# Running sums of eight groups from two float32r parts: GatedLoop attention with a SoLU feed-forward, one Trainium2 core

## The chip, the cores and the metric

The kernel runs on one core of one Trainium2 chip. The metric is the device time of a whole execution in microseconds (us). The time before is the median of three executions.

## The reference

For 4 batches, 8 heads, 768 steps and head dimension 48, a complex gate `a` is cut to a modulus of at most 0.999 and drives a linear recurrence; the real part of the state is read with `q`. The result (3072 tokens of 384) goes through a feed-forward block with a softmax-gated activation and a layer norm.

```python
scale = np.minimum(mag, 0.999) / (mag + 1e-06)
a_re_n, a_im_n = a_re * scale, a_im * scale
for t in range(S):
    new_re = ar * S_re - ai * S_im          # ar, ai: a_re_n, a_im_n at step t
    new_im = ar * S_im + ai * S_re
    S_re, S_im = new_re + k[t] (x) v[t], new_im
    y[t] = q[t] . S_re
h = x @ w_in                                # x: y, heads side by side; 3072x384 @ 384x1024
solu = h * softmax(h)
ln = (solu - mean) / sqrt(var + 1e-06) * g_ln
out = ln @ w_out                            # 1024x384
```

## The kernel before

The sequence is cut into 6 blocks of 128 steps. A block of one batch is a chunk; there are 24 chunks, numbered c, and two chunks of neighbouring batches are a group g, of which there are 12 (g counts from 0, so "group 5" of the title is g = 4). Within a block the recurrence is unrolled: the logarithm of the gate's modulus and its angle are summed along the 128 steps, which turns the recurrence into a masked product of scaled and rotated q and k.

The work is made of small named steps, and each is a closure that issues one or a few instructions:

- Preparation of a group, on tiles of 128 partitions by 768 (`prep_steps`): `inverse`, `ratio`, `sure`, `tangent`, `square`, `secant`, `fourth`, `size`, `eps` and `lnm` compute the tangent of the angle in tile `x0` and the logarithm in tile `lr`. They alternate between ScalarE (ACT) and VectorE (DVE). `total` then sums `lr` along the 128 steps by a matrix product with a triangle of ones (`tri`); `grow` and `decay` (ACT) take the exponential of the sum with both signs. After a load of the trigonometric table (`trig`), `angle` takes the arctangent, `on` (DVE) adds the phase carried over from the block before, and `phase` sums `x0` by a product with the triangle scaled by -0.5/pi (`turns`). `nearest`, `part`, `sin` and `cos` follow, and `exp` loads the exponential table again. `total` and `phase` are done for each chunk of the group (index 0 and 1). `ks` and `qs` scale k and q (DVE).
- Rotation of a chunk (`turn_steps`): `q2` and `k2` (DVE), a blockwise transpose `kqb` (DVE) and four DMAs `kqt0` that complete it.
- Attention of a chunk (`chunk_steps`): `score0/1` on TensorE (PE), `mask0` (DVE), `values` (PE), and `carry` (PE) with `add` (DVE) for the state.
- Feed-forward of a chunk (`ffn_steps`): `turned_x` (ACT copy), `up0/1` (PE), `exp0` (ACT), `solu0` (DVE), `blocks` (DVE transpose) and `away` (DMAs), `centred` (POOL, that is GpSimd), `spread` (ACT), `norm` (POOL), `down0/1` (PE), `scale` (ACT), `store` (DMA). Chunks 0, 1, 2 and 23 transpose with PE instead (`zt`, `zT`).
- Weights: `fetch`, `raised`, `convert` turn the 64-bit weights into float32; `again` fetches each of the seven pieces a second time and `inspect` (DVE) looks for values that are too small.

Nothing is scheduled at run time. A text, `ORDER`, lists all steps in one sequence, and each engine and the DMA queue on SyncE (SP) executes its own instructions in that order; semaphores bind the engines to each other. Tiles come from pools: the scratch tiles `lr`, `x0` and `u` have one buffer each, so the preparation of group g+1 can't overwrite them before group g has read them; the pool `raw`, which holds fetched weights, has three buffers; PSUM for `total`, `phase` and the transposes has two banks, and the accumulators f_y, f_h and f_o have one buffer each.

Every product has float32 operands. Most are cut into four instructions of 32 stationary columns that write 32 output partitions each, and the four run in the array side by side. The trace has two records of each float32 product. The running sums are issued so (line 846):

Of the kernel before, what the change touches and what calls it, by code (L numbers as in the profile page):

```python
# [11 lines left out]
FP = mybir.dt.float32  # L12
I32 = mybir.dt.int32
# [502 lines left out]
load_ara:0 inversea:0 load_aia:0 ratioa:0 surea:0 load_arb:0 tangenta:0 inverseb:0 squarea:0 load_aib:0 secanta:0  # L516
fourtha:0 ratiob:0 sureb:0 sizea:0 fetch:5 epsa:0 tangentb:0 squareb:0 secantb:0 lnma:0 fetch:1 raised:5 load_k:0
sizeb:0 fetch:0 epsb:0 total0:0 convert:5 load_q:0 fourthb:0 raised:1 grow0:0 decay0:0 lnmb:0 total1:0 grow1:0 fetch:2
decay1:0 convert:1 trig:0 anglea:0 angleb:0 ks1:0 phase0:0 phase1:0 load_vr:0 raised:0 convert:0 nearest0:0 nearest1:0
load_ar:1 part0:0 cosa:0 sina:0 qs0:0 qs1:0 load_ai:1 part1:0 ks0:0 sinb:0 fetch:6 cosb:0 q2:0 last:0 exp:0 qt0:0  # L520
qT0:0 raised:2 k2:0 qt1:0 qT1:0 kt0:0 kt1:0 load_v:0 q2:1 convert:2 kT0:0 inverse:1 fetch:3 fetch:4 gain:0 kT1:0 qt1:1
raised:6 k2:1 score0:0 onward:0 kt0:1 qT1:1 score1:0 turn_ends:0 ratio:1 kT0:1 load_k:1 sure:1 mask0:0 tot:0 tangent:1
values:0 convert:6 square:1 turned_x:0 secant:1 fourth:1 qt0:1 raised:3 size:1 convert:3 eps:1 qT0:1 load_q:1 lnm:1
up1:0 up0:0 raised:4 exp0:0 convert:4 total1:1 total0:1 grow1:1 ks1:1 decay0:1 grow0:1 decay1:1 trig:1 kt1:1 load_ar:2
angle:1 carry:1 kT1:1 phase0:1 ks0:1 load_ai:2 qs0:1 last:1 nearest0:1 solu0:0 phase1:1 nearest1:1 part0:1 score1:1
part1:1 score0:1 sin:1 mask0:1 zt1:0 qs1:1 cos:1 add:1 mean:0 load_q:2 mean:1 exp:1 mean:3 zT1:0 q2:2 values:1 k2:2
mean:7 inverse:2 load_v:1 mean:5 mean:4 mean:2 turned_x:1 mean:6 turn_ends:1 kqb:2 ratio:2 meansum:0 carry:0 up0:1
kqt0:2 centre:6 zt0:0 tot:1 sure:2 centred:0 centre:5 tangent:2 centre:7 square:2 up1:1 score0:2 score1:2 secant:2
spread:0 centre:4 centre:1 centre:0 size:2 zT0:0 k2:3 eps:2 centre:2 centre:3 down0:0 load_vr:1 fourth:2 q2:3 lnm:2
total1:2 exp0:1 total0:2 kqb:3 decay0:2 grow1:2 load_k:3 grow0:2 mask0:2 add:0 decay1:2 trig:2 down1:0 load_k:2  # L530
solu0:1 angle:2 on:2 values:2 kqt0:3 onward:1 zt0:1 centred:1 qs0:2 turned_x:2 zT0:1 carry:2 phase1:2 phase0:2 last:2
load_ar:3 nearest0:2 norm:0 score0:3 score1:3 ks1:2 nearest1:2 part0:2 scale:0 part1:2 sin:2 add:2 up1:2 cos:2
load_ai:3 up0:2 mask0:3 ks0:2 exp:2 q2:4 k2:4 inverse:3 values:3 exp0:2 load_v:2 turn_ends:2 load_q:3 zt1:1 kqb:4
ratio:3 zT1:1 solu0:2 turned_x:3 sure:3 down0:1 centred:2 tangent:3 kqt0:4 down1:1 tot:2 spread:1 square:3 zt1:2
secant:3 zt0:2 qs1:2 size:3 up1:3 carry:3 zT0:2 q2:5 k2:5 load_vr:2 fourth:3 eps:3 up0:3 store:0 norm:1 scale:1
score1:4 lnm:3 zT1:2 kqb:5 total1:3 add:3 total0:3 onward:2 exp0:3 load_ar:4 score0:4 down0:2 decay0:3 decay1:3
grow1:3 mask0:4 grow0:3 load_k:4 solu0:3 kqt0:5 qs0:3 centred:3 down1:2 blocks:3 spread:2 trig:3 angle:3 values:4 on:3
turned_x:4 phase1:3 phase0:3 last:3 norm:2 ks0:3 nearest0:3 carry:4 nearest1:3 part0:3 load_v:3 score1:5 ks1:3 away:3
part1:3 score0:5 add:4 up1:4 sin:3 cos:3 scale:2 qs1:3 exp:3 store:1 load_ai:4 spread:3 load_q:4 up0:4 mask0:5
turn_ends:3 inverse:4 q2:6 values:5 k2:6 kqb:6 exp0:4 ratio:4 turned_x:5 solu0:4 sure:4 tangent:4 down0:3 norm:3  # L540
kqt0:6 down1:3 centred:4 square:4 blocks:4 carry:5 secant:4 size:4 up1:5 tot:3 store:2 k2:7 eps:4 q2:7 scale:3 up0:5
score1:6 lnm:4 score0:6 onward:3 kqb:7 exp0:5 away:4 total1:4 load_vr:3 fourth:4 load_ar:5 total0:4 down0:4 decay0:4
solu0:5 grow1:4 grow0:4 mask0:6 decay1:4 trig:4 kqt0:7 centred:5 qs0:4 angle:4 down1:4 blocks:5 add:5 spread:4 on:4
store:3 values:6 away:5 phase0:4 last:4 turned_x:6 phase1:4 norm:4 ks0:4 nearest0:4 carry:6 nearest1:4 part0:4 part1:4
add:6 score0:7 sin:4 score1:7 ks1:4 up1:6 scale:4 up0:6 mask0:7 qs1:4 load_ai:5 turn_ends:4 spread:5 load_q:5 down0:5
cos:4 q2:8 values:7 exp:4 k2:8 inverse:5 kqb:8 exp0:6 ratio:5 load_k:5 down1:5 turned_x:7 solu0:6 sure:5 tangent:5
kqt0:8 carry:7 square:5 blocks:6 secant:5 norm:5 away:6 load_vr:4 fourth:5 up0:7 size:5 up1:7 k2:9 eps:5 q2:9
centred:6 score0:8 tot:4 score1:8 lnm:5 total0:5 kqb:9 scale:5 total1:5 load_v:4 exp0:7 decay0:5 down0:6 grow1:5
grow0:5 mask0:8 decay1:5 solu0:7 kqt0:9 qs0:5 down1:6 add:7 centred:7 spread:6 values:8 blocks:7 trig:5 angle:5
onward:4 on:5 last:5 phase0:5 turned_x:8 norm:6 phase1:5 away:7 ks0:5 nearest0:5 carry:8 nearest1:5 up1:8 part1:5  # L550
part0:5 store:5 scale:6 add:8 score0:9 sin:5 cos:5 score1:9 ks1:5 qs1:5 load_ar:6 load_ai:6 spread:7 load_q:6 up0:8
mask0:9 q2:10 values:9 exp:5 k2:10 kqb:10 down0:7 exp0:8 inverse:6 ratio:6 down1:7 turned_x:9 solu0:8 sure:6
turn_ends:5 kqt0:10 norm:7 tangent:6 square:6 blocks:8 store:4 carry:9 secant:6 size:6 up1:9 load_vr:5 fourth:6 up0:9
k2:11 tot:5 eps:6 q2:11 score0:10 centred:8 away:8 score1:10 lnm:6 exp0:9 total0:6 kqb:11 scale:7 total1:6 load_k:6
load_v:5 add:9 spread:8 decay0:6 down0:8 grow0:6 mask0:10 decay1:6 solu0:9 grow1:6 trig:6 kqt0:11 ks1:6 qs0:6 down1:8
centred:9 onward:5 values:10 blocks:9 away:9 angle:6 on:6 turned_x:10 norm:8 phase1:6 last:6 phase0:6 nearest0:6 ks0:6
part0:6 carry:10 nearest1:6 part1:6 up1:10 store:7 add:10 score0:11 sin:6 cos:6 score1:11 up0:10 mask0:11 scale:8
k2:12 q2:12 kqb:12 exp:6 load_ar:7 down0:9 load_ai:7 spread:9 load_q:7 exp0:10 inverse:7 ratio:7 values:11 down1:9
turned_x:11 sure:7 solu0:10 turn_ends:6 tangent:7 square:7 norm:9 blocks:10 qs1:6 kqt0:12 carry:11 secant:7 store:6
add:11 size:7 up1:11 load_vr:6 fourth:7 eps:7 up0:11 away:10 k2:13 q2:13 centred:10 score0:12 load_v:6 exp0:11 tot:6  # L560
score1:12 lnm:7 total0:7 kqb:13 scale:9 total1:7 grow1:7 decay0:7 down0:10 grow0:7 mask0:12 decay1:7 solu0:11 load_k:7
trig:7 angle:7 store:8 spread:10 qs0:7 centred:11 down1:10 kqt0:13 blocks:11 values:12 on:7 last:7 phase0:7
turned_x:12 norm:10 phase1:7 onward:6 scale:10 up1:12 carry:12 nearest1:7 nearest0:7 ks0:7 part1:7 away:11 part0:7
add:12 score0:13 sin:7 cos:7 score1:13 ks1:7 up0:12 mask0:13 exp:7 k2:14 q2:14 load_ar:8 load_ai:8 spread:11 kqb:14
load_q:8 exp0:12 inverse:8 ratio:8 down0:11 values:13 sure:8 down1:11 turned_x:13 solu0:12 kqt0:14 turn_ends:7
tangent:8 square:8 blocks:12 qs1:7 onward:7 secant:8 carry:13 norm:11 store:10 away:12 size:8 up1:13 load_vr:7
fourth:8 k2:15 q2:15 eps:8 up0:13 score0:14 centred:12 tot:7 scale:11 exp0:13 score1:14 lnm:8 total1:8 total0:8 kqb:15
grow1:8 decay0:8 down0:12 load_v:7 grow0:8 mask0:14 decay1:8 solu0:13 load_k:8 load_ar:9 kqt0:15 centred:13 qs0:8
spread:12 down1:12 add:13 trig:8 values:14 store:11 angle:8 turned_x:14 blocks:13 norm:12 on:8 away:13 store:9 last:8
phase0:8 phase1:8 ks0:8 nearest0:8 load_ai:9 spread:13 carry:14 nearest1:8 part0:8 up1:14 load_q:9 part1:8 score1:15  # L570
ks1:8 add:14 score0:15 sin:8 cos:8 norm:13 exp:8 up0:14 mask0:15 k2:16 scale:12 q2:16 down0:13 kqb:16 exp0:14
inverse:9 ratio:9 values:15 down1:13 turned_x:15 solu0:14 sure:9 turn_ends:8 kqt0:16 tangent:9 square:9 blocks:14
qs1:8 secant:9 carry:15 scale:13 up1:15 size:9 load_vr:8 fourth:9 eps:9 up0:15 q2:17 k2:17 centred:14 score0:16 tot:8
# [37 lines left out]
def whole(ctx, tc, flag, q, k, v, a_re, a_im, moe_w_in, moe_w_out, moe_g_ln, out):  # L611
# [179 lines left out]


    def prep_steps(g):
        ti, b0 = g * GB // B, g * GB % B

        class Tiles(dict):
            def __missing__(self, nm):
# [138 lines left out]
        if ti > 0:  # L936
            own["on"] = on
        if ti < NC - 1:
            own.update(turn_ends=turn_ends, tot=tot, onward=onward)
# [379 lines left out]
```

## Time and profile before

| | |
|---|---|
| Time, median of 3 | 422.66 us (422.07 to 425.59) |
| Profiled execution, its own time | 421.44 us |
| Its span | 419.1 us |
| PE busy | 381.9 us (91%) |
| DVE busy | 331.8 us (79%) |
| ACT busy | 287.5 us (69%) |
| POOL busy | 57.0 us (14%) |
| Running sums on PE (line 848), busy | 38.4 us |

The profile is of one execution. A busy time is the union of an engine's instructions; "PEld" is the load of the stationary operand, which runs beside the products. Instruction groups are named by source line, engine, operation and tile (output<-inputs). `f_L` is the output of `total`, `f_phase` that of `phase`, `f_h` of `up`, `f_o` of `down`, `f_y` of `values`, `f_d` of `carry`, `f_zt` of the transposes on PE. The shape "128*32" of a product means 128 rows by 32 columns of the stationary operand.

### The profile page before, as it was taken

Reading aid. Unit: us, or ns where it says so; the run is one execution under the profiler, and the core shown is the slowest. Engines: PE = TensorE matmul, PEld = TensorE weight load, DVE = VectorE, ACT = ScalarE, POOL = GpSimd, SP = SyncE. Lnnn points to the kernel's source line nnn. Section 1 sums busy time; section 2 is a strip of 40 time slices with the busy share of each in tenths; the row PEclk is TensorE's granted clock in tenths of the full one; section 3 lists DMA queues with packets and bytes.
Section 4 is the critical chain, followed back from the end, with each engine's and each line's share of the span. In section 5 each row is a group of like instructions: output and inputs, shape, how many; then the busy total and the mean of one; then the engine's idle time right before and its main releaser. Section 6 shows DMA issues by size and latency. Waiting matters only on the chain.

```text
span 419.1 us, 15795 instructions
## 1 busy us (share of the span) xinstructions
PE 381.9 (91%) x6928; PEld 200.4 (48%) x6928; DVE 331.8 (79%) x429; ACT 287.5 (69%) x468; POOL 57.0 (14%) x139
## 2 busy tenths in 40 slices
PE   0258779999999999999999999999999999999993
PEld 0025344555554554554555555555455544545441
DVE  4899899788799689699699599689798798774550
ACT  5898978888577768677667767866866885621440
POOL 3000000321210201021211211102111111010210
PEclk9988999999999999999999999999999999999998
DMA  8999436875858738769589857788868869478970
GB/s 235 311 262 215 86 83 127 180 159 113 194 137 173 176 93 179 151 149 206 122 191 201 176 125 157 189 180 192 167 141 196 167 156 204 94 170 256 328 260 28
DMA packets 167261, 72.58 MB, mean 173 GB/s; under 512 B 142480, under 2 KB 155792, under 8 KB 166416
## 3 DMA queue, kind: packets, MB, share of 16 engines
q1 hardware_dynamic: 167040, 71.17, 72.3%
q8 instruction: 56, 0.92, 0.9%
q10 hardware_dynamic: 144, 0.33, 0.3%
q14 instruction: 21, 0.17, 0.1%
HBM read 38.87 MB, written 4.72 MB: 104 GB/s over the span
## 4 chain that ended last, share of the span: by engine, by line
PE 79%; ACT 9%; DMA 4%; DVE 3%; issue 2%; SPq 0%; POOL 0%; DVEq 0%; ACTq 0%; POOLq 0%
PE f_o L1162 28%; PE f_h L1085 26%; PE f_y L1044 9%; PE f_score L1011 5%; PE f_phase L848 4%; PE f_L L848 4%; PE f_d L1052 3%; DMA f_ar<-in_a_re_dram 2%; DMA f_raw<-in_moe_w_out_dram 1%; DMA f_kqT<-f_kb 1%; PE f_zt L1112 1%; ACT f_cs L912 1%; ACT L946 1%; DVE f_kb L966 1%; ACT f_cs L907 1%
## 5 line engine op out<-in xcount | busy, mean ns | idle before, releaser
L1085 PE MATMUL f_h<-f_w_in,f_xT 128*32 128x512 f32 x1152 | 130.7, 593 | 0.4 <-ACT f_xT L1078 0.4
L1162 PE MATMUL f_o<-f_w_out,f_zT 128*32 128x384 f32 (+1 forms) x1344 | 130.1, 486 | 0.3 <-ACT f_zT L1117 0.2
L1162 PEld LDWEIGHTS f_o<-f_w_out,f_zT 128*32 128x32 f32 (+1 forms) x1344 | 55.0, 114 | 64.9 <-issue 55.0
L1085 PEld LDWEIGHTS f_h<-f_w_in,f_xT 128*32 128x32 f32 x1152 | 39.7, 110 | 64.8 <-issue 64.0
L966 DVE STREAM_TRANSPOSE f_kb<-f_kq 128x1536 f32<-128x1536 f32 x22 | 56.0, 2544 | 2.6 <-DMA f_kqT<-f_kb 2.2
L1095 ACT ACTIVATE f_z<-f_h 128x1024 f32<-128x1024 f32 x24 | 28.6, 1193 | 15.5 <-PE f_h L1085 15.5
L1078 ACT COPY f_xT<-f_y 128x384 f32<-128x384 f32 x24 | 11.4, 474 | 39.8 <-PE f_y L1044 39.8
L1011 PEld LDWEIGHTS f_score<-f_kqT 96*32 96x32 f32 x1536 | 32.7, 111 | 10.4 <-issue 9.8
L1044 PE MATMUL f_y<-f_att,f_v 128*32 128x128 f32 (+1 forms) x384 | 36.1, 273 | 1.2 <-DVE f_att L1016 1.2
L1104 DVE SCALAR_TENSOR_TENSOR f_z<-f_h,f_z 128x1024 f32<-128x1024 f32 (+1 forms) x36 | 33.4, 962 | 3.9 <-ACT f_z L1095 3.9
L1044 PE MATMUL f_y<-f_att,f_vr 128*32 128x128 f32 x384 | 36.4, 273 | 0.0
L1140 POOL TENSOR_SCALAR f_less<-f_sum 128x1 f32<-128x1 f32 x24 | 13.1, 546 | 163.4 <-DVE f_z L1104 152.7
L1016 DVE TENSOR_TENSOR f_att<-f_score,f_mats 128x1024 f32<-128x1024 f32 x24 | 29.1, 1213 | 7.2 <-PE f_score L1011 7.2
L903 DVE SCALAR_TENSOR_TENSOR f_f<-f_f,f_phase 128x384 f32<-128x384 f32 x24 | 13.0, 552 | 26.8 <-ACT f_f L899 26.5
L848 PE MATMUL f_L<-f_lr,f_mats 128*32 128x384 f32 x192 | 19.3, 518 | 15.7 <-DVE f_lr L843 15.7
L1011 PE MATMUL f_score<-f_kqT 96*32 96x32 f32 (+3 forms) x1536 | 32.8, 236 | 0.0
L1044 PE MATMUL f_y<-f_kqT,f_state 96*32 96x128 f32 (+1 forms) x640 | 32.7, 272 | 0.0
L1143 ACT ACTIVATE f_z<-f_z,f_less 128x1024 f32<-128x1024 f32 x24 | 27.5, 1147 | 0.0
L1166 ACT ACTIVATE f_ot<-f_o,f_rs 128x384 f32<-128x384 f32 x24 | 13.7, 573 | 16.5 <-POOL f_rs L1151 6.0
L1044 PEld LDWEIGHTS f_y<-f_att,f_v 128*32 128x32 f32 (+1 forms) x384 | 21.8, 103 | 6.2 <-issue 3.8
L1122 DVE STREAM_TRANSPOSE f_zb<-f_z 128x1024 f32<-128x1024 f32 x20 | 24.8, 1238 | 0.1
L957 DVE TENSOR_TENSOR f_kq<-f_cs,f_q 128x768 f32<-128x768 f32 x24 | 22.9, 952 | 2.2 <-ACT f_cs L912 1.1
(101 smaller groups left out, 585.2 us busy)
## 6 DMA issues: line engine op xcount, KB each, us to landing
f_kqT<-f_kb SPq DMA_DIRECT2D x88, 192.0 KB, 3.4
f_zT<-f_zb SPq DMA_DIRECT2D x80, 128.0 KB, 3.2
f_raw<-in_moe_w_out_dram SPq DMA_DIRECT2D x16, 384.0 KB, 5.1
f_raw<-in_moe_w_in_dram SPq DMA_DIRECT2D x6, 1024.0 KB, 7.7
f_k<-in_k_dram SPq DMA_DIRECT2D x12, 384.0 KB, 5.2
f_q<-in_q_dram SPq DMA_DIRECT2D x12, 384.0 KB, 5.4
f_v<-in_v_dram SPq DMA_DIRECT2D x12, 384.0 KB, 5.0
out_dram<-f_ot SPq DMA_DIRECT2D x24, 192.0 KB, 3.7
```

Of the source, the lines that this page charges most:

```text
L848: nc.tensor.matmul(out=ps[r:r + 32], lhsT=weights[:, r:r + 32], rhs=st[nm][:, i * DM:(i + 1) * DM], start=True, stop=True)
L957: nc.vector.tensor_tensor(out=t, in0=T["cs", g][:, i * H:(i + 1) * H], in1=heads(T[nm, g][:, i]).unsqueeze(2).to_broadcast([P, H, 2, D]), ...
L966: nc.vector.transpose(out=t, in_=T["kq", c].rearrange("p n h (f j) -> p j (n h) f", j=3))
L1011: nc.tensor.matmul(out=scores[r0:r0 + 32, x, r:], lhsT=QK[:, r // 32, x], rhs=QK[:, r // 32:, H + x], start=True, stop=True)
L1016: nc.vector.tensor_tensor(out=st["att"].rearrange("p (i u) t -> p i u t", u=2), in0=scores.rearrange("p (i u) t -> p i u t", u=2), in1=mat ...
L1044: nc.tensor.matmul(**product)
L1085: nc.tensor.matmul(out=st["h"][r:r + 32, half * 512:(half + 1) * 512], lhsT=st["xT"][:, c * P + r:c * P + r + 32], rhs=w_in[:, c, half * 5 ...
L1095: nc.scalar.activation(out=z, in_=h, func=AF.Exp, accum_out=sums[:, n:n + 1])
L1104: nc.vector.scalar_tensor_tensor(out=z, in0=h, scalar=1.0, in1=z, op0=OP.mult, op1=OP.mult, accum_out=st["sum"][:, 2 + i:3 + i])
L1122: nc.vector.transpose(out=st["zb"], in_=st["z"].rearrange("p (c s f) -> p s c f", s=4, f=32))
L1143: nc.scalar.activation(out=st["z"], in_=st["z"], func=AF.Square, bias=st["less"], accum_out=st["sum"][:, 1:2])
L1162: nc.tensor.matmul(out=st["o"][rows], lhsT=zT, rhs=w_out[:, c], start=(c == 0), stop=(c == KF - 1))
```

## The change

For the groups g = 4 to 11 the summed tile is split into two parts in the type float32r, and each running sum is one product of the whole 128-column triangle with the first part and a second that accumulates the rest, in place of four products of 32 columns in float32. Both sums use the triangle of ones; the factor -0.5/pi of the phase goes into the split. `lh` and `xh` make the first part on ACT, into the buffer of `u`; `ll` makes the rest of the logarithm on POOL and `xl` that of the phase on DVE, both into buffers of `raw`. Groups 0 to 3 are computed as before. `ORDER` is written anew over its whole length: two of the repeated fetches of weights (`again:5` and `again:0`) stand early, `load_ai` of a group stands ahead of `load_ar`, and most steps keep their neighbours or move by a few places. On PE a group's steps stand in the same sequence as before, except that a `score` comes ahead of `carry` after each `phase`.

```diff
+FR = mybir.dt.float32r
...
+        split = g >= 4
...
+        def high(nm, src, by):
+            t = st[nm] = tmp.tile([P, GW], FR, tag="u", name="f_" + nm)
+            nc.scalar.activation(out=t, in_=st[src], func=AF.Copy, scale=by)
+
+        def low(nm, src, hi, by):
+            t = st[nm] = rawp.tile([P, 1024], FR, tag="raw", name="f_" + nm)
+            if by == 1.0:
+                nc.gpsimd.tensor_tensor(out=t[:, 0:GW], in0=st[src], in1=st[hi].bitcast(FP), op=OP.subtract)
+            else:
+                nc.vector.scalar_tensor_tensor(out=t[:, 0:GW], in0=st[src], scalar=by, in1=st[hi].bitcast(FP), op0=OP.mult,
+                                               op1=OP.subtract)
+
+        def halves(ps, i, *parts):
+            for k, nm in enumerate(parts):
+                nc.tensor.matmul(out=ps, lhsT=tri.bitcast(FR), rhs=st[nm][:, i * DM:(i + 1) * DM], start=(k == 0),
+                                 stop=(k == len(parts) - 1))
...
-            running(ps, i, tri, "lr")
+            if split:
+                halves(ps, i, "lh", "ll")
+            else:
+                running(ps, i, tri, "lr")
...
-            running(ps, i, turns, "x0")
+            if split:
+                halves(ps, i, "xh", "xl")
+            else:
+                running(ps, i, turns, "x0")
...
+        if split:
+            c = -0.5 / math.pi
+            own.update(lh=partial(high, "lh", "lr", 1.0), ll=partial(low, "ll", "lr", "lh", 1.0),
+                       xh=partial(high, "xh", "x0", c), xl=partial(low, "xl", "x0", "xh", c))
```

One period of the order, from one `exp` to the next, as each engine sees it, for g = 9:

```
before
ACT  exp:8 scale:12 exp0:14 inverse:9 turned_x:15 sure:9 square:9 secant:9 scale:13 fourth:9 eps:9 tot:8 exp0:15
     grow0:9 decay0:9 grow1:9 decay1:9 trig:9 angle:9 spread:14 turned_x:16 nearest0:9 nearest1:9 part0:9 scale:14
     part1:9 sin:9 spread:15 cos:9 exp:9
DVE  mask0:15 k2:16 q2:16 kqb:16 ratio:9 solu0:14 tangent:9 blocks:14 qs1:8 size:9 q2:17 k2:17 lnm:9 kqb:17 mask0:16
     solu0:15 qs0:9 add:15 blocks:15 on:9 ks0:9 part0:9 part1:9 add:16 ks1:9 mask0:17 k2:18 q2:18
POOL centred:14 centred:15 norm:14
PE   up0:14 down0:13 values:15 down1:13 turn_ends:8 carry:15 up1:15 up0:15 score0:16 score1:16 total1:9 total0:9
     down0:14 down1:14 values:16 phase0:9 phase1:9 carry:16 up1:16 score0:17 score1:17 up0:16
after
ACT  exp:8 spread:13 inverse:9 exp0:14 sure:9 turned_x:15 square:9 secant:9 fourth:9 eps:9 lh:9 spread:14 scale:13
     tot:8 exp0:15 grow0:9 decay1:9 decay0:9 grow1:9 trig:9 angle:9 xh:9 turned_x:16 nearest0:9 nearest1:9 part0:9
     part1:9 sin:9 cos:9 scale:14 exp:9
DVE  mask0:15 k2:16 q2:16 kqb:16 ratio:9 solu0:14 tangent:9 blocks:14 qs1:8 size:9 k2:17 lnm:9 q2:17 kqb:17 add:15
     mask0:16 solu0:15 on:9 blocks:15 xl:9 qs0:9 ks0:9 ks1:9 part0:9 part1:9
POOL norm:13 centred:14 ll:9 norm:14 centred:15
PE   down0:13 values:15 down1:13 turn_ends:8 carry:15 up1:15 score1:16 up0:15 score0:16 total1:9 total0:9 down0:14
     down1:14 values:16 phase0:9 phase1:9 score0:17 carry:16 score1:17 up0:16
```

## The prediction

> **What bounds the kernel now.** I read the engine totals, then the clock row, then busy time by stretch, then the chain of waits in order of time.
>
> ```profile
> span 419.1 us, 15795 instructions
> PE 381.9 (91%) x6928; PEld 200.4 (48%) x6928; DVE 331.8 (79%) x429; ACT 287.5 (69%) x468; POOL 57.0 (14%) x139
> ...
> PEclk9988999999999999999999999999999999999998
> ```
>
> The stretches, columns PE, PEld, DVE, ACT, POOL:
>
> ```profile
> 100.00:405.00 305.00, 304.81 (x5877) 160.11 (x5866) 243.68 (x293) 201.27 (x327) 43.97 (x104) 1.00 0.75 176
> 405.00:419.00 14.00, 6.82 (x30) 3.90 (x26) 3.97 (x9) 3.30 (x6) 1.80 (x7) 0.91 0.15 51
> ```
>
> From 100 to 405 us PE is idle for 0.2 us, at full clock. Work taken off PE there is time off the end, provided nothing else becomes late. The chain (start, duration) gives the price of a running sum and of a change of tile shape:
>
> ```profile
> 86.24 0.59 PE f_zt L1112 x4
> 86.82 5.16 PE f_o L1162 x16
> 91.99 0.87 PE f_zt L1112 x8
> 92.86 2.71 PE f_h L1085 x24
> ...
> 101.23 5.36 PE f_o L1162 x16
> ...
> 118.81 5.16 PE f_o L1162 x64
> ...
> 130.91 1.29 PE f_L L848 x16
> ```
>
> A pair of sums (both chunks) costs 1.29 us in the steady part, 0.645 us each: 384 columns at four array cycles each, at the 2.4 GHz that the Trainium skill's "TensorE: Matmul & The Clock Gate", Part 1, gives for a busy array. The f_o of 16 records is the 128-column shape, that of 64 the four-tile shape; both take 5.16 us, so a 128-column load hides. The eight transposes of 128 columns take 0.87 us, 0.109 us each, so it hides even there. Entering the wide shape from tiles costs about 0.2 us (5.36 against 5.16; 0.59 against 0.43 for four transposes), leaving it 0.13 us (2.71 against 2.58).
>
> How close the preparation is to being late is read from the timeline at the logarithm's end (L843) and the sum that follows:
>
> ```profile
> 127.55 0.96 DVE L843 SCALAR_TENSOR_TENSOR f_lr<-f_lr,f_u 128x768 f32<-128x768 f32 x1 [0.24 <-ACT f_u L840]
> 130.73 1.47 PE L848 MATMUL f_L<-f_lr,f_mats 128*32 128x384 f32 x16
> ...
> 283.63 0.96 DVE L843 SCALAR_TENSOR_TENSOR f_lr<-f_lr,f_u 128x768 f32<-128x768 f32 x1 [0.39 <-ACT f_u L840]
> 284.64 1.50 PE L848 MATMUL f_L<-f_lr,f_mats 128*32 128x384 f32 x16
> ```
>
> Over the eight groups the slack between the two is 2.2, 1.1, 0.6, 0.05, 0.6, 0.05, 1.0 and 0.5 us, 0.76 in the mean. From the end of `on` (L891) to `phase` it is 0.2 to 1.9 us. PE is the bound, but the preparation is a second chain just under it. DVE (16 of 20 us) and ACT (13 of 20) have room in sum.
>
> **What the Trainium skill says.** "FP8 and Floating Point Precision", TensorE Precision Notes: true float32 takes four passes, while the reduced form reads 4 bytes and truncates to 22 bits. The four cycles a column above agree with the first; no trace here shows the second. I estimate from it one pass, 384 / 2.4 = 0.16 us a product. "TensorEngine Tiling (Array Packing)", Key Properties: a change of tiling mode drains the array; the 0.2 and 0.13 us above agree. "GPSIMD Engine Reference", 3.1: a float32 tensor_tensor of 2048 elements takes 4497 ns; scaled to 768, I estimate 1.69 us for `ll`. "SBUF — State Buffer", "SBUF: two separate sides": GpSimd and a DVE instruction with two SBUF inputs exclude each other. The trace agrees: POOL's L1150 took 1.56 us at 291.66, against 0.22 elsewhere, while DVE ran L891 and L872, both of two inputs, until 293.15.
>
> **The change part by part.**
>
> *Products.* 8 groups x 2 = 16 pairs. Removed: 16 x 1.29 = 20.6 us. Added per pair: four products of 0.16 us = 0.64, plus one entry and exit, 0.33, together 0.97; 16 x 0.97 = 15.5 us. Saved: 5.1 us; I take 4.9, since entering in the middle of a group cost 0.24 once (f_o at 68.12, after scores). Bounds: at half the entry cost, 7.5 us saved; if a float32r column takes two cycles and not one, a pair is 1.29 + 0.33 and 5.3 us are lost.
>
> *`lh`, `ll` ahead of `total`.* `lh` is an ACT pass over 128x768, 0.84 us (row L826); `ll` 1.69 us on POOL, bounded by 0.95 (the same shape on DVE, L836) and 3.0 (1.69 plus the 1.34 that L1150 waited). With 0.1 for semaphores that is 2.6 us in a chain with 0.76 to spare, so it must start earlier. In g = 9 the old table load ends at 269.13, but `inverse` starts at 271.56, behind `scale`, a wait for f_h of 0.82 and `exp0`; `ratio` waits 1.19 for the DMA of f_ai. In the new order only `spread` (1.14) is between, and f_ai is loaded ahead of f_ar: about 2.5 us regained, `lnm` done near 282.1, `lh` 283.0, `ll` 284.7. PE arrives 0.3 us earlier than before, 284.3, and reaches the second part 0.36 us later. It just fits. Behind `ll` on POOL stands `norm`, which `scale` needs only before the next `down` pair, over 5 us later.
>
> *`xh`, `xl` ahead of `phase`.* After `lh` ACT has `spread`, `scale`, `tot` and `exp0` (2.9 us), so `grow` starts near 285.9; four exponentials take 1.64, the table 1.28, `angle` 0.85, `on` 0.9, `xh` 0.84. `blocks` (1.24, on DVE behind `on`) ends after that, then `xl` 0.96: ready near 292.7. PE, after 0.97 + 5.16 + 1.76 and the first part, is there at 292.55. A wait of 0.15 us a group, 1.2 us in all. Behind the waiting product on PE stand `score`, `carry` and `up`, everything. If the cover is gone, each late us is paid in full, because the next preparation starts only after this `phase` has freed `x0` and `u`. Other groups have other neighbours; I bound this wait by 0 and 0.8 us a group.
>
> *DVE and ACT load.* 0.96 and 1.7 us more per group of 30.7 us, on 25 and 22: hidden in sum.
>
> *Raw buffers.* `ll` and `xl` use two of three while `again:5` holds the third until late: the pair is free again after its product, a group earlier than needed. Nothing.
>
> *Head and tail.* Groups 0 to 3 compute the same; the first 60 us (PE idle for half of them, the DMA share 0.95 and 0.99 in the first 40) have a new order with the same transfers. I take 0, within 2 us either way. At the end `judges` (L1208 to L1210, 0.45 us at 402.33) now stands behind `solu0:23` instead of ahead, and two of seven repeated fetches are gone: 0.5 us gained, 0 if `down:22` covers it.
>
> Sum: -4.9 + 1.2 - 0.5 = -4.2; 421.44 - 4.2 = 417.2. The profiled execution is 0.3% under the median of 422.66; the same 4.2 from the median is 418.5, and I put the forecast at 417.3. Under 1%, 4.2 us, a measurement of this kernel can't be told from no change.
>
> **The rivals.**
>
> 1. *The main line*, 415 to 420, chance 0.45. For it: PE idle 0.2 of 305 us. A third of it lies over 418.4, the 1% bound.
> 2. *The new order does better*: shape changes at half price (another 2.6 us) and a shorter head (1 to 2): 413. Chance 0.12. For it: the head has 30 us of PE idling. Against: it is tied to transfers.
> 3. *The preparation becomes the bound*: 0.6 us a group of waiting at `phase` rather than 0.15. -4.9 + 4.8 - 0.5: 420.8. Chance 0.22. For it: the slacks of 0.05 us. Against: idle of ACT at the old `inverse`.
> 4. *The other side: `ll` is slow.* Place: POOL between `lnm` and `total`. If it takes 3.2 us, held out by `k2`/`q2` on DVE, PE waits 1.5 us at each of eight totals, which `phase` passes on: -4.9 + 12 - 0.5 = +6.6: 428. It decides from 2.2 us on, where the wait of 0.5 with that at `phase` eats the saving. Chance 0.13, from 422.5 to 430.
> 5. *float32r isn't a single pass*: +5.3 + 1.2 - 0.5: 427.4. Chance 0.08. The loss would lie in the products themselves, with no waits.
>
> **How the numbers follow.** Faster by over 1%: 0.30 + 0.12 + 0.08 (the part of 3 whose head is short) = 0.50. Within 1%: 0.15 + 0.14 = 0.29. Slower: 0.13 + 0.08 = 0.21. The range 411.5 to 426.5 holds 1 to 3 and the near half of 4. The likeliest case's own range is 415 to 420.
>
> **What would show it.** Right: f_L and f_phase of the split groups as records of 128*128 with starts 0.16 us apart, a pair near 0.97 us in the chain, periods between phases near 30.1 us instead of 30.7. Wrong: PE waits on POOL's `ll` (4), on DVE's `xl` (3), products twice as long (5). A head that ends elsewhere than near 60 us would mean that the order and not the split moved the time.

## The result, and the profile after

The changed kernel takes 421.81 us in the median (420.46 to 424.49), against 423.0 us for the kernel before in the same series (421.04 to 428.58). The ratio is 0.997, 95% interval 0.9948 to 0.9992: a gain of about 0.3%, below the 1% that I asked of a change to be told from none. The profiled execution took 421.55 us, 0.1 more than that of before.

Engine totals and clock row of the changed kernel:

```profile
span 419.7 us, 15441 instructions
...
PE 381.2 (91%) x6736; PEld 207.8 (50%) x6736; DVE 339.8 (81%) x437; ACT 301.0 (72%) x484; POOL 70.7 (17%) x147
...
PEclk9956999999999999999999999999999999999999
```

PE lost 192 records (6928 to 6736) and 0.7 us of busy time, where the sums alone should have given 4 to 5. The clock row has a 5 and a 6 in its first tenth, where before had two 8s: the trace's clock records (when the granted clock changed, and to what share) have it at half for 17.1 us there, and for 6.8 us before. The stretch from 100 to 405 us, columns PE, PEld, DVE, ACT, POOL, then the granted clock:

```profile
100.00:405.00 305.00, 304.77 (x5752) 167.43 (x5748) 255.81 (x298) 218.17 (x350) 58.48 (x111) 1.00 0.76 177
```

PE is idle for only 0.2 us, as before, though DVE has 12 and ACT 17 us more to do there: no wait for `ll` or `xl`. The chain of waits (start, duration) has the new pairs:

```profile
136.37 0.90 PE f_L L863 x4
137.28 5.30 PE f_o L1192 x64
...
144.33 0.90 PE f_phase L863 x4
```

A pair takes 0.90 us instead of 1.29, and the f_o behind it 5.30 instead of 5.16. The two rests that feed it, by form (busy us, mean ns of one, then idle before them):

```profile
L856 POOL TENSOR_TENSOR f_ll<-f_lr,f_lh 128x768 fp32r<-128x768 f32 x8 | 15.5, 1933 | 53.9 <-ACT f_lh L851 53.9
L858 DVE SCALAR_TENSOR_TENSOR f_xl<-f_x,f_xh 128x768 fp32r<-128x768 f32 x8 | 7.2, 903 | 0.0
```

I cut the span at the phase sums of groups 1, 3 and 11 (start of the first record in the timeline). Before: 50.16, 108.30, 353.83, end 419.1. After: 51.78, 113.73, 355.15, end 419.7.

| part of the span, us | before | after | difference |
|---|---|---|---|
| start to phase of g = 1 | 50.16 | 51.78 | +1.62 |
| g = 1 to g = 3 (the middle of the head) | 58.14 | 61.95 | +3.81 |
| g = 3 to g = 11 (all the split sums but the last `phase` pair) | 245.53 | 241.42 | -4.11 |
| g = 11 to the end (the tail) | 65.27 | 64.55 | -0.72 |

So the part that the sums were to shorten is shorter by about the amount forecast, and the head, in which groups 0 to 3 compute the same as before, has lost it again. Busy time by stretch from 60 to 115 us, first of the kernel before (a stretch not shown so far):

```profile
60.00:115.00 55.00, 54.92 (x895) 30.14 (x898) 46.72 (x70) 42.54 (x68) 10.30 (x20) 1.00 0.71 155
```

and then of the changed kernel:

```profile
60.00:115.00 55.00, 51.24 (x754) 27.27 (x754) 45.09 (x65) 38.87 (x64) 6.95 (x19) 1.00 0.67 151
```

Before, PE was full there; now it idles for 3.8 us. The chain in this part of the changed kernel:

```profile
68.87 2.80 PE f_o L1192 x8
...
72.77 0.64 ACT f_ai L835
74.54 1.98 ACT f_z L1125 x2
77.62 1.28 ACT L973
78.91 0.85 ACT f_x L909
79.79 0.95 DVE f_x L914
80.79 1.54 PE f_phase L868 x16
...
89.60 1.91 ACT f_z L1125 x2
91.99 5.43 PE f_o L1192 x16
```

From 72.77 to 80.79 and again up to 91.99 the chain runs over ACT, where in the kernel before it stayed on PE. PE's waits give two of the four terms (us in total, times, longest):

```profile
PE f_o L1192 <- ACT f_ot L1196: 1.7, 1, 1.7
PE f_phase L868 <- DVE f_x L914: 1.2, 1, 1.2
```

The other two from 60 to 115 us are 0.6 us at f_mean and 0.3 us at f_zt; together they are the 3.8 us.

### The profile page after: what moved, and what is told of

The parts are those of the page before. It is cut to its first block, busy times and chain, and to the rows that moved or that the text cites. A ratio compares the mean times of both kernels' runs of the same rounds, so it can differ in the third digit from the quotient of the medians.

```text
span 419.7 us, 15441 instructions
## 1 busy us (share of the span) xinstructions
PE 381.2 (91%) x6736; PEld 207.8 (50%) x6736; DVE 339.8 (81%) x437; ACT 301.0 (72%) x484; POOL 70.7 (17%) x147
## 4 chain that ended last, share of the span: by engine, by line
PE 84%; ACT 10%; issue 2%; DVE 2%; DMA 1%; POOL 0%; SPq 0%; DVEq 0%; POOLq 0%
PE f_h L1115 29%; PE f_o L1192 28%; PE f_y L1074 9%; PE f_score L1041 6%; PE f_d L1082 3%; PE f_L L863 2%; PE f_phase L863 2%; ACT f_z L1125 1%; PE f_phase L868 1%; DMA f_ar<-in_a_re_dram 1%; PE f_turned L1008 1%; PE f_parts L772 1%; ACT f_bits L748 1%; ACT L973 1%; PE f_L L868 1%
## 5 line engine op out<-in xcount | busy, mean ns | idle before, releaser
L1115 PEld LDWEIGHTS f_h<-f_w_in,f_xT 128*32 128x32 f32 x1152 | 41.0, 110 | 65.9 <-issue 63.8
L1074 PE MATMUL f_y<-f_att,f_v 128*32 128x128 f32 (+1 forms) x384 | 37.4, 275 | 0.0
L1041 PE MATMUL f_score<-f_kqT 96*32 96x128 f32 (+3 forms) x1536 | 34.5, 239 | 0.8 <-ACT f_kqT L1014 0.8
L1179 POOL TENSOR_SCALAR f_s<-f_s,f_sum 128x1 f32<-128x1 f32 x24 | 9.5, 396 | 133.8 <-ACT f_z L1173 132.7
L1074 PEld LDWEIGHTS f_y<-f_att,f_v 128*32 128x32 f32 (+1 forms) x384 | 22.8, 104 | 8.8 <-issue 7.8
L856 POOL TENSOR_TENSOR f_ll<-f_lr,f_lh 128x768 fp32r<-128x768 f32 x8 | 15.5, 1933 | 53.9 <-ACT f_lh L851 53.9
L1074 PEld LDWEIGHTS f_y<-f_att,f_vr 128*32 128x32 f32 x384 | 22.9, 111 | 1.7 <-issue 1.6
```

The costliest lines, as they stand in the source:

```text
L1041: nc.tensor.matmul(out=scores[r0:r0 + 32, x, r:], lhsT=QK[:, r // 32, x], rhs=QK[:, r // 32:, H + x], start=True, stop=True)
L1074: nc.tensor.matmul(**product)
L1115: nc.tensor.matmul(out=st["h"][r:r + 32, half * 512:(half + 1) * 512], lhsT=st["xT"][:, c * P + r:c * P + r + 32], rhs=w_in[:, c, half * 5 ...
```

## The experiments

The theory: the split sums save about 4 us, and the rewritten order gives them back between 45 and 115 us, by a few steps that ACT and PE now meet in another sequence. The rivals: the saving isn't one of the sums; the loss lies in the first transfers, or in the early repeats; or the 1.6 and 3.8 us are chance of one execution. In the fragments of the order below, a minus line is the changed kernel's. Line numbers of these kernels are lower by one than those of the changed kernel, or by a few more.

Parts of the span as above, from one profile each, and the medians (n runs), with the ratio to the kernel before and its 95% interval. The runs were made in several series; the kernel before, measured with each, had medians of 422.8 to 423.5 us, so small differences between runs are better read from the ratios. "Full clock from" is read from the clock records of each trace: from then on PE's granted clock is 1.00, but for the stretches named behind it, up to 115 us, which are at 0.50. What stands before it is taken up under "The first 50 us".

| run | to g=1 | g=1 to 3 (to 2) | g=3 to 11 | tail | full clock from | median (n) | ratio |
|---|---|---|---|---|---|---|---|
| before | 50.16 | 58.14 (27.23) | 245.53 | 65.27 | 34.2 | 423.0 (22) | |
| changed | 51.78 | 61.95 (29.01) | 241.42 | 64.55 | 39.3 | 421.81 (22) | 0.997, 0.9948 to 0.9992 |
| order_only | 51.67 | 61.95 (29.00) | 246.06 | 68.22 | 38.8 | 429.19 (6) | 1.0114, 1.0072 to 1.0156 |
| split_old_order | 53.15 | 58.18 (27.27) | 264.45 | 64.52 | 43.5 | 442.19 (6) | 1.0421, 1.0372 to 1.0469 |
| head_120 | 50.74 | 61.91 (28.97) | 241.35 | 64.60 | 35.6 | 421.16 (22) | 0.9954, 0.993 to 0.9978 |
| head_before | 53.19 | 58.19 (27.28) | 253.46 | 64.56 | 43.5 | 428.28 (9) | 1.0098, 1.0064 to 1.0133 |
| head_before2 | 49.63 | 58.88 (27.97) | 241.43 | 66.46 | 30.6; 54.5 to 57.9 | 419.95 (22) | 0.993, 0.991 to 0.9949 |
| mid_before | 51.80 | 58.19 (27.28) | 241.59 | 66.62 | 39.4 | 421.87 (22) | 0.9974, 0.9954 to 0.9995 |
| again_late | 52.29 | 62.65 (29.71) | 241.14 | 67.92 | 40.1; 50.3 to 53.7 | 424.05 (22) | 1.0021, 1.0 to 1.0043 |
| scale_early | 52.05 | 61.27 (29.97) | 241.51 | 64.57 | 40.4; 50.7 to 54.1 | 419.69 (22) | 0.993, 0.9911 to 0.9949 |
| exp0_early | 51.59 | 61.86 (28.92) | 241.81 | 64.64 | 38.4 | 422.0 (16) | 0.9975, 0.995 to 1.0001 |
| turn_early | 51.54 | 61.80 (28.87) | 241.32 | 64.74 | 38.8 | 421.94 (22) | 0.9979, 0.996 to 0.9997 |
| two_moves | 51.62 | 60.15 (28.80) | 241.80 | 64.63 | 38.8 | 420.29 (9) | 0.993, 0.9904 to 0.9956 |
| two_turn_scale | 50.22 | 60.12 (28.84) | 241.17 | 64.59 | 31.3 | 420.46 (22) | 0.994, 0.992 to 0.9961 |
| three_moves | 51.84 | 58.95 (27.52) | 241.47 | 64.54 | 39.4 | 419.72 (6) | 0.9909, 0.9872 to 0.9945 |
| best_head | 53.41 | 58.18 (27.27) | 241.67 | 65.34 | 43.8 | 419.42 (6) | 0.9883, 0.9841 to 0.9925 |
| best_mid | 51.03 | 60.68 (29.77) | 242.30 | 65.49 | 37.5; 51.2 to 54.6, 58.0 to 61.4 | 419.99 (9) | 0.9919, 0.9893 to 0.9945 |
| warm | 50.17 | 58.98 (28.08) | 241.96 | 64.79 | 34.8; 55.3 to 58.7 | 417.99 (11) | 0.9903, 0.9872 to 0.9934 |
| warm_three | 51.07 | 58.95 (27.52) | 241.47 | 64.51 | 37.2 | 418.91 (6) | 0.9896, 0.9859 to 0.9933 |
| before, once more | 50.67 | 58.93 (28.02) | 246.65 | 65.25 | 35.2; 55.7 to 59.1 | 423.6 (1) | |

**Sums and order apart.** The order without the sums:

```diff
-        split = g >= 4
+        split = False
```

> The changed written order, with the sums of all groups left in float32 as before (no lh, ll, xh, xl). Theory H: the head's 5 us lost and no gain of 4 us from the sums: about 426, 1% above the changed kernel and 0.7% above the kernel before, with the pairs f_L and f_phase back at 1.29 us and periods of 30.7 us. Rival S: 421 to 423, as the changed kernel; then the order and not the split made the steady part shorter.

Measured 429.19 us. Its chain has the old pairs, and a period of 30.64 us where the changed kernel has 30.10:

```profile
136.23 1.29 PE f_L L867 x16
144.44 1.29 PE f_phase L867 x16
```

From g = 3 to 11 it takes 4.6 us more than the changed kernel; 0.9 of it is one period of 31.57 us, in which no wait of PE is seen. Its middle is that of the changed kernel to 0.01 us. So the saving belongs to the sums, once the steady part is in the new order, and the loss to the order. The total is 3 us worse than expected: its tail takes 3.7 us more than the changed kernel's, some 0.3 of which is the last pair; 1.4 us is a stand of PE for which the trace has no releaser. Why stays open.

The sums without the order: before's sequence, with the four new steps at the first place where they can stand.

```diff
+ lnm:g lh:g ... ll:g total ... on:g xh:g ... xl:g phase
```

> The kernel before's whole written order with the float32r sums put in where they are first possible: lh behind lnm, ll just ahead of total, xh behind on, xl just ahead of phase, for groups 4 to 11. If the steady part's new order is needed, PE waits for lh and ll at each total (2.6 us more of a chain that had 0.76 us to spare, so about 1.9 us) and for xh and xl at each phase (some 1 us): 8 x 2.9 = 23 us less the 4 saved, 435 to 442 us. Rival R (the reordering of the steady part is not needed; PE's other work covers it): 417 to 419, the short head of the kernel before with the saving of the sums.

Measured 442.19 us. PE's waits from 100 to 405 us:

```profile
PE f_L L862 <- POOL f_ll L855: 9.0, 7, 1.5
PE f_phase L862 <- ACT f_xh L850: 4.0, 3, 1.4
PE f_L L862 <- ACT f_lh L850: 1.8, 2, 0.9
PE f_phase L862 <- DVE f_xl L857: 1.7, 3, 0.6
```

16.5 us of waiting at the sums, instead of none, out of the 23.0 that it takes more than the changed kernel from g = 3 to 11. Of the rest the trace shows two stretches of 3.4 us at half clock (from 231.2 and 265.3 us), which the changed kernel doesn't have; what remains isn't listed by this view. The steady part had to be written anew for the split to pay, and there the new order works.

**Where in the head.** After 120 steps both orders have issued the same set, so they can be joined there; and after 368 steps of the old one nearly so.

```diff
+ # head_120:    old[:120] + new[120:]
+ # head_before: old[:368] + what is left of new
```

> The changed kernel with only its first 120 steps (through total1:1, the first 45 us) in the order of the kernel before; after 120 steps both orders have issued the same set. Theory H splits the head's 5.4 us by the milestones: 1.5 us are lost before the second group's phase, the rest later, between 77 and 106 us. So about 1.5 us less than the changed kernel, near 420.3. Rival T (all of the head's loss follows from how the first transfers are ordered, since what is late at 45 us pushes everything behind it): near 417.

421.16 us, 0.65 less than the changed kernel, and a middle of 61.91: the 3.8 us are not a consequence of how the first 45 us are ordered. Rival T falls.

> The changed kernel with the first 368 steps of the written order taken from the kernel before (through carry:5, into group 4), and the changed order from there on; the float32r sums of groups 4 to 11 are kept. Theory H (the sums saved about 4 us in the steady part, and the new order's head gave 5 us back): phase of group 3 near 108.5 us instead of 113.9, periods of 30.1 us after it, total about 417 us, 1.2% under the changed kernel. Rival S (the head's delay is taken up again later, or the saving in the steady part isn't one of the sums): total within 2 us of the changed kernel, 420 to 424 us.

428.28 us, 11 more than expected, though the middle took 58.19 us, as the old order should. What DVE and PE waited for between 105 and 145 us:

```profile
DVE f_least L760 <- DMA f_raw<-in_moe_w_in_dram: 9.3, 1, 9.3
...
PE f_L L862 <- ACT f_lh L850: 8.3, 1, 8.3
```

That is my seam: the changed order has again:0 and inspect:0 early, so they fell right behind the joint, and inspect stood on DVE ahead of group 4's logarithm until its megabyte had come. From 139.1 to 149.3 us the clock was at half besides. The run says nothing on the head; the next two move these steps to the end.

> head_before once more, with again:5, again:0 and inspect:0 moved to the end, so that no inspect stands in DVE's queue ahead of group 4's logarithm. Theory M: the seam's 12 us are gone; from phase of group 1 to phase of group 3 58.3 us, periods of 30.1. The total depends on when TensorE runs up: with the first up at 5.36 us near 416.7, with it at 6.76 near 419.7; so a median of 417 to 419.5 with a wider spread than mid_before. Rival G: 421 to 422.

419.95 us: 1.9 us less than the changed kernel, though just above the 417 to 419.5 expected. The middle takes 58.88 us, 0.7 of which is the stretch at half clock (see below).

> The changed kernel's first 120 steps, then the kernel before's steps 121 to 368 (45 to 115 us: the second sums of groups 1 to 3 and the preparation between them), then the changed order; the repeats again:5, again:0 and their inspect go late, as in the kernel before. Theory M (the middle of the head is where the new order loses: from phase of group 1 to phase of group 3 the three runs with the new order there took 62.1 us and those with the old one 58.3): phase of group 3 near 110.1 us and a total near 418, 3.8 us under the changed kernel. Rival A (it is the early repeats that delay the middle): the same 418, but again_late alone then gives it too. Rival G (what is gained by 110 us is lost at the seam with the changed order): 421 to 422.

The middle is 58.19 us, as theory M has it, but the median is 421.87 us, as the rival has it. Both kernels have a tail of 66.5 us. again_late, the changed kernel with nothing else moved, shows why:

> The changed kernel with again:5, again:0 and inspect:0 alone moved to the end. Theory M: they are transfers that collide with little, 421 to 422, within 1 us of the changed kernel, and 62 us from phase of group 1 to phase of group 3. Rival A: the two megabyte loads in groups 1 and 3 are the head's loss, near 418.

424.05 us, worse by 2.2. The middle doesn't get shorter (62.65 us, with a stretch at half clock; from g = 2 to 3, at full clock, 32.94 as in the changed kernel), so the early repeats don't delay it. But at the end DVE waits for the last repeat, 5.00 us:

```profile
413.35 2.94 DVE L760 TENSOR_REDUCE f_least<-f_raw 128x1 f32<-128x768 f32 x3 [5.00 <-DMA f_raw<-in_moe_w_out_dram]
```

and PE 2.4 us for the count behind it:

```profile
PE f_count L1243 <- DVE f_row L1233: 2.4, 1, 2.4
```

In the new order's tail, the early repeats are worth 2 to 3.4 us. The profile of mid_before (420.04 us) has the changed kernel's clock records to 0.1 us up to 115 us, and is 1.5 us shorter: 3.8 won in the middle, 2.1 lost in the tail. That its median gains nothing at all is more than this explains, and stays open.

**Which steps.** In the changed kernel the copy f_ot on ACT starts at 91.36, behind a table load and exp0. One move:

```diff
- inverse:3 zt1:1 exp0:2 scale:0 kqb:4
+ part1:2 add:2 scale:0 sin:2 cos:2
```

> The changed kernel with one step moved: scale:0 (ACT's write of the first output tile, which frees the PSUM tile that down of group 1 waits for) stands ahead of sin:2 again, as in the kernel before, instead of behind exp0:2. If the 1.66 us that f_o waited for f_ot at 91.99 is all its own: 420.2. If the steps behind are late anyway (ACT takes the same work in another order): 421.8, no change.

419.69 us, 2.1 under the changed kernel (1.7 by the ratios), and the wait of f_o for f_ot is gone. Its part from g = 1 to 2 is 1 us longer, with a stretch at half clock in it; from g = 2 to 3 the clock is full in all traces, and there the step is seen alone: 31.30 us instead of 32.94. The six profiles of the new order there with scale:0 late (changed, order_only, head_120, again_late, exp0_early, turn_early) have 32.93 to 32.95 us, the five with it early 31.28 to 31.43, and the nine with the old order 30.90 to 30.91. The copy now runs ahead of the sines:

```profile
86.15 0.56 ACT L1195 ACTIVATE f_ot<-f_o,f_rs 128x384 f32<-128x384 f32 x1
```

For the late phase of group 2, one step at a time:

```diff
- total0:2 values:2 decay1:2 grow0:2 exp0:1 load_ai:3
+ exp0:1 total0:2 values:2 decay1:2 grow0:2 load_ai:3
```

> The changed kernel with one step moved: exp0:1 (two ACT passes for the output path, 2.1 us with their accumulator reads) stands ahead of total0:2 again, as in the kernel before, and no longer between the exponentials of group 2, where on:2 and then phase of group 2 waited for it (1.23 us at 80.79). If that wait is exp0's own: phase of group 2 1.2 us earlier and 420.6. If the angle was late by another cause: 421.8.

422.0 us: nothing. ACT's timeline shows why:

```profile
72.41 0.17 ACT L905 COPY f_tot<-f_tot 96x16 f32<-96x16 f32 x1 [2.00 <-PE f_tot L901]
...
73.32 2.17 ACT L1124 ACTIVATE f_z<-f_h 128x1024 f32<-128x1024 f32 x1
```

ACT stands at tot:1 for 2.0 us, because PE has its source, turn_ends:1, behind down0:0 and score1:2. exp0 can't use the time.

> The changed kernel with both steps back: scale:0 ahead of sin:2 (alone it gave 2.1 us) and exp0:1 ahead of total0:2. If these two moves are the middle's 3.8 us: phase of group 3 about 59 us after that of group 1, 418.3 us. If the rest of the changed order (the means, the second up pair, kqt on the queue) has a share of its own: 419 to 420.

420.29 us, a middle of 60.15: the gain of scale:0, and none of exp0:1.

```diff
- onward:1 down0:0 score1:2 add:0 turn_ends:1 eps:2
+ onward:1 turn_ends:1 down0:0 score1:2 add:0 eps:2
```

> The changed kernel with one PE step moved: turn_ends:1 (six small transposes that tot:1 on ACT copies from PSUM) stands ahead of down0:0 again instead of behind down0:0 and score1:2. In the changed kernel ACT stands at tot:1 for 2.0 us until 72.6, with the decay, the table load and the angle of group 2 behind it. Theory T (that wait is what makes phase of group 2 late): phase of group 2 1.3 us earlier, a total near 420.5. Rival E (the angle is late by something else, as it was when exp0 was moved): 421.8, no change.

421.94 us: nothing either. (The sequence of PE's steps, which the steady part keeps but for `score`, had changed here: before had turn_ends:1 ahead of down0:0.) The wait at tot:1 is gone, ACT waits for the sum itself instead, and exp0 still lies between the exponentials:

```profile
73.08 0.49 ACT L882 ACTIVATE f_ar<-f_L 128x384 f32<-128x384 f32 x1 [1.76 <-PE f_L L867]
...
74.05 2.08 ACT L1124 ACTIVATE f_z<-f_h 128x1024 f32<-128x1024 f32 x1
```

> The changed kernel with turn_ends:1 ahead of down0:0 and scale:0 ahead of sin:2. Theory T: the two waits (1.3 and 1.7 us) are separate and add: from phase of group 1 to phase of group 3 59.1 us instead of 62.1, a total near 418.5. Rival E: as scale_early, 419.7.

420.46 us and 28.84 us to the phase of group 2: as the rival has it. After two single moves without effect the theory was that each hides the other. three_moves makes all three; exp0:1 stands a little earlier than in exp0_early, ahead of total1:2 and fourth:2:

```diff
- lnm:2 total1:2 fourth:2 mask0:2 total0:2 values:2 decay1:2 grow0:2 exp0:1
+ lnm:2 exp0:1 total1:2 fourth:2 mask0:2 total0:2 values:2 decay1:2 grow0:2
```

> The changed kernel with three steps back where the kernel before has them: scale:0 ahead of sin:2, exp0:1 ahead of the totals of group 2, turn_ends:1 ahead of down0:0. Theory T2 (phase of group 2 is late by exp0's 2.1 us between the exponentials, and moving exp0 alone gave nothing because ACT then stood at tot:1 for the same 2.0 us, as moving turn_ends alone gave nothing because exp0 stayed; both are needed): from phase of group 1 to that of group 2 27.5 us instead of 28.9, to that of group 3 58.8 instead of 61.3 to 62.1; a total of 418.6. Rival E (a third cause): 28.9 again, and a total of 420, as two_turn_scale and two_moves.

To the phase of group 2 27.52 us (27.5 expected), to that of group 3 58.95 (58.8). The copy of tot and exp0 now fill the time in which ACT would wait for the sum:

```profile
70.56 0.15 ACT L905 COPY f_tot<-f_tot 96x16 f32<-96x16 f32 x1
70.61 2.19 ACT L1124 ACTIVATE f_z<-f_h 128x1024 f32<-128x1024 f32 x1
...
73.56 0.49 ACT L882 ACTIVATE f_ar<-f_L 128x384 f32<-128x384 f32 x1
```

The profiled execution took 418.6 us, as expected. Up to 115 us its clock records are those of the changed kernel's profile to 0.1 us, and it is 3.0 us shorter, all of it in the middle. Seven profiles of the changed order at full clock have 28.80 to 29.01 us from g = 1 to 2; this one and warm_three have 27.52. Two_turn_scale differs from it in exp0:1 alone, so that exp0:1 is worth 1.3 us once turn_ends:1 is early is shown. That turn_ends:1 is needed too is shown less strictly, since two_moves has exp0:1 at the later place; but in exp0_early ACT stands at tot:1, which is ahead of both places, until 72.41. The median of six runs is 419.72, no better than scale_early's, so in the medians the gain of the last two moves isn't shown: only the trace has it.

The wait of 0.6 us at f_mean is the only one that PE has left from 60 to 115 us, where the middle is still 0.8 us longer than 58.14 to 58.19, what the old order takes at full clock.

**The first 50 us.** Seven profiles that begin with the old 120 steps (warm apart) reach the phase of group 1 at anything from 49.63 to 53.41 us. Look at the first up (f_h) in the timeline; of the kernel before, in its second profile:

```profile
39.37 5.36 PE L1085 MATMUL f_h<-f_w_in,f_xT 128*32 128x512 f32 x48 [0.36 <-ACT f_xT L1078]
```

of best_head:

```profile
40.75 6.83 PE L1114 MATMUL f_h<-f_w_in,f_xT 128*32 128x512 f32 x48
```

In best_head, as in head_before and split_old_order, the same 48 records take 6.8 us instead of 5.36. The clock row of best_head is at 9 there, but that is no measurement: its trace has no clock record before 43.76 us, and the row prints a stretch without a record as full. What the clock was, the products tell. In all 20 traces the float32 products of f_L (128x384, 32 columns) take 482 to 511 ns where the clock is recorded at 1.00 (1344 of 1344 records), and 844 to 850 ns before the first clock record (319 of 319); those of f_phase, of the same shape, take 841 to 848 ns where it is recorded at 0.50 (44 of 44). So PE runs at half speed until the first record. In best_head that was until 43.76 us, 3.0 us into the up, which half speed then makes 1.5 us longer: 6.86 by this sum, 6.83 measured.

The Trainium skill, "TensorE: Matmul & The Clock Gate", Part 1, has this state: an array that stood idle runs at 1.2 GHz, and goes to 2.4 after a busy window, with windows that run freely, so that the same kernel comes up at different times in different runs. The traces agree: they have the clock at 1.00 and 0.50 only, from one change to the next it takes 3.41 us or a whole multiple of that, and half the pace fits the up just reckoned. A single record's duration grows by 1.7 only (486 to 847 ns), less than the 2 of that page.

Sorted by "full clock from", the seven starts with the old 120 steps fall into order: 30.6 us goes with 49.63 us to the phase of g = 1, 35.2 with 50.67, 43.8 with 53.41. Those with the new 120 steps follow the same line within 0.5 us.

The clock falls back for 3.4 us between 50 and 61 us in some traces too. Stretch 55 to 60 us of the kernel before, first and second profile (the clock is the third number from the end):

```profile
55.00:60.00 5.00, 3.68 (x56) 2.04 (x56) 4.96 (x6) 4.27 (x8) 0.00 (x0) 1.00 0.00 0
...
55.00:60.00 5.00, 4.24 (x48) 2.65 (x48) 4.96 (x7) 4.45 (x6) 0.00 (x0) 0.66 0.00 0
```

From g = 1 to 2 the old order takes 27.23 to 28.08 us, and best_mid 29.77. The five profiles without such a stretch have 27.23 to 27.28; one stretch adds 0.7 to 0.9 us (before once more, head_before2, warm), the two of best_mid 2.5. Again_late and scale_early have one stretch as well and are 0.7 and 1.0 us above the changed kernel.

> The kernel before once more, for a second profile of its head. If its head varies by itself (theory W), phase of group 1 is either near 50.2 us with an up of 5.36 us, as in the first profile, or near 53.2 with one of 6.8, as in three of the profiles that have its first 120 steps; from phase of group 1 to phase of group 3 58.3 us in both. If the head of this kernel is fixed and only the changed ones vary: 50.2 again, with no way to tell it from chance.

50.67 us with an up of 5.36, as in its first profile, so that one kernel does both isn't shown. But its clock records differ from those of the first profile (full from 35.2 instead of 34.2 us, and a stretch at half from 55.7): when the clock changes varies between executions of one kernel.

best_head joins the old head to the new rest with the repeats early; warm adds to it two products that nobody reads:

```diff
+            if g == 0 and i == 1:
+                spare = ps_t.tile([P, DM], FP, tag="t", padded_shape=[P, 512], name="f_spare")
+                for _ in range(2):
+                    nc.tensor.matmul(out=spare, lhsT=ones, rhs=mats[:, 0:3].rearrange("p n t -> p (n t)"), start=True, stop=True)
```

> The kernel before's first 368 steps, the changed order from there, and the repeats again:5 and again:0 with inspect:0 early, as the changed kernel has them. The run with the repeats at the end had a wait of 1.9 us of the last count for their inspect; that goes: head_before2's 419.95 less 1.9 = 418.0 us, faster than both kernels. If the early repeats cost in the head what they save in the tail: 420.

> best_head with two more products of constants, read by nobody, on PE between phase and the first transposes of group 0 (23.9 to 26.5 us, where PE waits 3.3 us for DVE). Theory W (TensorE still runs at half speed at 30 us because the idle before it; when it runs up decides 3 us of the head): the transposes at 27 us take half as long, the first up takes 5.36 us in the profile and is done by 44.5, phase of group 1 at 50 or before, a total of 416 to 417.5 and no more slow starts. Rival N (the head's time is set by ACT and DVE, PE's speed there does nothing): 419.4, as best_head.

best_head took 419.42 us; the tail is 1.1 us shorter than head_before2's, not 1.9. warm took 417.99 us. In its profile the transposes at 27.13 us take 1.05 us for eight instead of 1.91, and the phase of group 1 comes at 50.17 against 53.41 us. But a stretch from 31.4 to 34.8 us is at half speed again, and best_head's spread (417.04 to 420.6) overlaps warm's (417.09 to 421.84). That the two products brought the full clock isn't shown: warm has it first at 24.5 us, but so have the kernel before (24.0) and head_before2 (23.8) without them. Nor is it shown that they shorten the median.

> mid_before with the repeats early in the same way: the wait of 2.2 us of count goes, 421.87 - 2.2 = 419.7 us by the medians; by the profiled execution, 420.04 - 2.2 = 417.9. The first 120 steps of the changed order against those of the kernel before are then best_mid against best_head: 1.7 us if the medians are right, none if TensorE's run-up alone decided.

419.99 us; the tail is 65.49. It is 0.6 us above best_head, so the 1.9 us between the medians of mid_before and head_before2 aren't seen again. Its 29.77 us from g = 1 to 2 hold two stretches at half clock.

> three_moves with the two spare products of warm in group 0. Theory W (as in warm): the first up near 39 us instead of 40.4, phase of group 1 near 50.2, a total 1 to 1.5 us under three_moves, near 417.3 and faster than both kernels. Rival N: no change against three_moves.

418.91 us: 0.8 under three_moves in the median and in the profile (51.07 against 51.84 to the phase of group 1, with the clock full from 37.2 instead of 39.4 us; all else equal), with overlapping ranges. That the spare products did this isn't shown either. best_head, warm, warm_three and three_moves are all faster than both kernels, by 0.9 to 1.2% against the kernel before. Which of the four is best can't be told.

## Why the prediction was wrong

*What bounds the kernel* was right: PE stood for 0.2 us from 100 to 405 us, and work taken off it there came off that part.

*Products.* Forecast 0.97 us a pair, saving 4.9 us. Measured 0.90 + 0.14 = 1.04 us, 0.25 saved, 16 x 0.25 = 4.0 us. The products start 0.17 to 0.18 us apart, not 0.16, and entry with exit costs 1.04 - 4 x 0.175 = 0.34 us, as I had it. The term was mis-sized by the spacing. I had it from an estimate of one column a cycle; each part also loads 128 columns in 0.188 us beside it, and that may set the spacing, which no run tested. Rival 5 is out.

*The wait at `phase`*, 1.2 us: it is 0. I had `xl` start behind `blocks` and end at 292.7; in the run PE had no wait at a split sum at all. It was close: by the trace `xl` ended 0.1 to 0.6 us ahead of its pair, `ll` 0.1 to 0.6 us. Products and wait together were forecast at -3.7 and gave -4.1 (against order_only -4.6): two misses of opposite sign, so that the sum came near is luck. Rival 3 is out.

*`ll` on POOL*: 1.69 us forecast, 1.93 in the mean (seven of 1.85 to 1.86, one of 2.49). The mean is under the 2.2 us from which rival 4 decided, and it was started early enough. Split_old_order shows the wait that rival 4 had in mind, by another way: where `ll` isn't slow (1.81 to 1.84 us) but starts late, PE waits 9.0 us for it.

*Tail*: -0.5 forecast, -0.7 measured, some 0.25 of which is the last `phase` pair and belongs to the products. The mechanism, fewer repeats at the end, is worth more in the new order: without it 2 to 3.4 us are lost (again_late, mid_before). That the tail as a whole came near the forecast is luck, then; what else in the new order's tail costs time wasn't looked for.

*Head*: this is the step that failed: "I take 0, within 2 us either way". I looked at the first 60 us, where PE stands half of the time and transfers set the pace. There the mean of seven profiles with the old 120 steps is 51.56 us to the phase of group 1, that of eleven with the new 51.58: zero was right as far as these runs can tell. The 1.62 us belong to the two executions that I compared first, in which the clock was full from 34.2 and from 39.3 us. From 60 to 115 us PE is already the bound (54.92 of 55 us busy), and there I didn't follow the order. Three moved steps made ACT late twice. scale:0 behind exp0:2 costs 1.6 us (scale_early). exp0:1 between the exponentials of group 2, with turn_ends:1 behind down0:0, costs 1.5 us (three_moves, 29.01 to 27.52). With both undone 58.95 us are left, against 58.14 to 58.19 with the old order at full clock; of these 0.8 us, 0.6 stand at f_mean, and no run moved that.

The whole by parts: 0 for the start, +3.8 for the middle, -4.1 and -0.7: -1.0 us; the medians moved by -1.2. A smaller part of the miss is the base: the sum of -4.2 gives 418.5 from the median, as the prediction says, and I put down 417.3, which is the same sum from the profiled execution. Without the middle the changed kernel would be at some 418.0. My test in the profile, that the head should end near 60 us, stood at the wrong place: most of the loss came after it.

One reading was wrong without effect: ACT was busy for 20.3 us of a group's 30.7 before (201.27 of 305 us), not 22.

Rival 2, a shorter head in the new order, went the other way: the head got longer.

## What to carry to other kernels

When a change brings a new written order, cut the span at a few fixed instructions and compare part by part before you give the total to the edit: here +3.8 and -4.1 us made "no change". Follow the moved steps through every stretch where the bounding engine is full, also where nothing is computed otherwise; a step moved on ACT by a few places held TensorE for 1.6 us. Compare the clock records of two traces before you compare their parts: half clock moved this kernel's parts by 0.7 to 3.8 us, as much as the change itself, and the clock row prints a stretch without a record as full. A single move that gives nothing doesn't clear the step: here two waits of 2 us on the same engine stood behind each other, and the gain came when both were moved.

## What the hardware showed that I had not expected

The same TensorE instructions ran 1.7 times slower (847 against 486 ns for 128x384 in float32) at the start. From 30.6 to 43.8 us on, depending on the profile, the clock was full up to 50 us; in six of the 20 profiles it was at half again for 3.4 us at a time between 50 and 61 us. When the clock changes differs between executions, and a spread of 3.8 us goes with it in the start (49.63 to 53.41 us to the phase of group 1 with the same 120 steps).

A float32r product of 128 columns by 384 costs 0.175 us where it follows another, and its first record on entering from 32-column tiles takes 0.44 us instead of 0.34.
